# Batching the key transposes and scores ahead of the value product, and moving the projection pieces to even units, in a cached GQA decode kernel

## The chip, the cores and the metric

One core of one Trainium2 (trn2) chip. The metric is the device time of one execution in microseconds (us). A profile's span is about 2 us shorter than the time of the same run (before: 453.79 us and a span of 451.5).

Engines in the profile: PE is TensorE (matmul), PEld its weight loads, DVE VectorE, ACT ScalarE, POOL GpSimd, SP SyncE, which issues the loads. "Warm" and "cold" (or "half clock") stand for a granted TensorE clock of 1.00 and of 0.50 in the windows view of the profile.

## The reference, cut to what matters

Two attention blocks of one decode step stand side by side. Block A attends over 8192 cached positions; block B only over the last 2048.

```python
def block(x, k_cache, v_cache, wq, wo):         # B: caches cut to the last W = 2048 positions
    q = (x @ wq) -> [4 batch, 32 heads, 1, 128]
    k, v = caches [4, 8 kv heads, S, 128], each kv head shared by 4 query heads
    scores = q . k * 128 ** -0.5
    p = softmax(scores)                          # over positions
    return (p . v) reshaped to [4, 1, 4096] @ wo # -> [4, 1, 512]
out = concatenate([block(A), block(B)], axis=-1)
```

This is grouped-query attention (GQA): query heads share a kv head. About nine tenths of the bytes are K and V: 184.56 MB are read per execution.

## The kernel before

The work is cut into 20 units, 0 to 19. A unit owns one 4 MB piece of K and one 4 MB piece of V, in two-slot buffers. TensorE transposes K in 16 steps `T`, and VectorE and ScalarE evict the transposes in turn. TensorE then forms scores in 16 steps `S`, three steps behind. The softmax of unit u-1 is finished during unit u, and so are its row sums `SM` and its value product, 8 chunks `PV` of 16 matmuls. So `PV` inside unit u needs V of unit u-1. Two units make one turn of a loop on TensorE. In seven turns an output projection piece (`OT`, `OL`, `OPJ`; 1 MB of `wo`) is done in the turn's odd unit; the last piece is done after the loop. In the first three turns the same instructions run and their result is not used.

```python
LA, PV0 = 3, 10
TOK = []; pc = 0
for k in range(NJ + LA):                       # NJ = 16
    if k < NJ: TOK.append(("T", k))
    if k >= LA: TOK.append(("S", k - LA))
    if k == PV0 - 1: TOK.append(("SM",))
    if k >= PV0 and pc < NC:                   # NC = 8
        TOK.append(("PV", pc)); pc += 1
AFTER = {("S", 2): ("OT",), ("S", 5): ("OL",), ("S", 8): ("OPJ",)}

for u in range(NU):                            # NU = 20, unrolled for all engines but TensorE
    turn[0] = tn = u // 2
    odd = u % 2 == 1                           # this unit carries the projection piece
    # ... cut: TensorE ops in the order of TOK; PV 0 waits for V of unit u - 1 ...
    for k in range(0, NJ, 2):                  # VectorE, in order
        add(ev[k])                             # eviction of transpose k
        if k == 0 and u >= 1:
            add(dve_submask(u - 1)); add(dve_sub(u - 1, 0))
        if k == 2 and u >= 1: add(dve_sub(u - 1, 1))
        # ... cut ...
        if k == 12 and u >= 1: add(dve_sum(u - 1)); add(dve_rcp(u - 1))
    add(dve_max(u, 1))                         # ... cut: maxc, addmask; POOL all-reduce ...
    if u >= 1: add_norm(u - 1)                 # waits for the last PV chunk
# tail, L = NU - 1 = 19
add(dve_submask(L)); add(dve_sub(L, 0)); add(dve_sub(L, 1)); add(act_exp(L))
op("pe", pe_seed, ...)                         # puts the output so far into two PSUM banks
pe_SM(L)
# ... cut: PV of unit 19 (V comes in 4 chunks), norm, last projection with Wl, store ...

# SyncE: order of loads; each waits until its buffer slot is free
for u in range(1, NU + 1):
    if u < NU: kv_load("K", u)                 # waits for T 15 of unit u - 2
    kv_load("V", u - 1)                        # waits for the last PV of unit u - 3
    if u % 2 == 0 and u // 2 in pieces: load of Wo   # waits for the OPJ of the turn before
```

## Time and profile before

| | before |
|---|---|
| time, median of 3 runs | 453.9 us (453.87 to 454.83) |
| span of the profile | 451.5 us |
| PE busy | 81% |
| DMA queue of the loads, share of 16 engines | 96.3% |

From the page of the kernel before: the DMA busy share and the traffic in 40 equal slices of the span (11.3 us each; digits are tenths), and the line of the queue that carries all loads (packets, MB, share).

```profile
DMA  8999999999999999999999999999999999999950
GB/s 358 406 414 421 420 418 420 422 446 430 422 430 441 427 425 427 436 432 424 430 434 431 427 441 425 427 427 431 437 424 427 437 434 422 433 439 424 409 192 2
...
q1 hardware_dynamic: 12944, 184.56, 96.3%
```

Here is the tail in the timeline of the kernel before. Its columns are start, duration, engine, line, operation, output<-inputs, shapes, count; in brackets is the idle time before it and what ended it. On TensorE, `KT<-identf,K_sb` are transposes of K, `SA` or `SB<-RQc,KT_sb` scores, `SA<-PT,onesb` row sums, `OT<-PT,V_sb` value chunks (`KT<-PT,V_sb` in unit 19's own value product) and `KT<-Wo_sb,OL` a projection piece.

```profile
416.64 3.42 PE L257 MATMUL KT<-identf,K_sb 128*128 128x128 f32 x16 [4.42 <-DMA K_sb<-in_A_k_cache_dram]
...
426.51 0.63 PE L304 MATMUL OT<-PT,V_sb 128*128 128x64 bf16 x16
...
427.72 1.89 PE L367 MATMUL KT<-Wo_sb,OL 128*4 128x512 bf16 x8
...
435.44 0.63 PE L304 MATMUL OT<-PT,V_sb 128*128 128x64 bf16 x16
...
435.90 0.35 PE L290 MATMUL SB<-RQc,KT_sb 128*128 128x16 bf16 x8
436.28 0.69 DVE L396 TENSOR_REDUCE M<-SB 128x8 f32<-128x512 f32 x1 [2.63 <-PE SB L290]
...
438.08 0.69 DVE L434 TENSOR_TENSOR Dt<-SA,MBm 128x512 f32<-128x512 f32 x1
...
439.40 1.06 ACT L443 ACTIVATE PT<-Dt 128x1024 bf16<-128x1024 f32 x1 [4.28 <-DVE Dt L434]
...
440.51 0.78 PE L316 MATMUL SA<-PT,onesb 128*128 128x64 bf16 x16 [2.10 <-ACT PT L443]
...
441.10 5.33 PE L304 MATMUL KT<-PT,V_sb 128*128 128x64 bf16 x128
```

Unit 19 starts when its K lands (416.64). Its first value chunk comes at 426.51, a projection piece at 427.72, the last value chunk at 435.44 and the last scores at 435.90. Only then comes the serial softmax chain: maximum, two subtractions, exponential (to 440.46), the last row sums (440.51) and the last 128 value matmuls. From the waits of TensorE (total us, times, longest):

```profile
PE KT L257 <- DMA K_sb<-in_A_k_cache_dram: 29.5, 7, 4.5
...
PE OT L304 <- DMA V_sb<-in_A_v_cache_dram: 3.8, 5, 1.5
```

### The profile page before, as it was taken

The numbers are of one execution on the slowest core, as the hardware profiler recorded it, in microseconds if no ns is written. First come the engines' busy times: TensorE is split into PE (matmuls) and PEld (weight loads), VectorE is DVE, ScalarE is ACT, GpSimd is POOL, SyncE is SP. The second block draws the span as 40 slices with busy tenths as digits, with TensorE's granted clock in tenths as the row PEclk, the third lists the DMA queues.
The fourth block names the chain that finished last, engine by engine and source line by source line (L and its number), as shares of the span: only waits on it lengthen the run. The fifth ranks groups of instructions, "written<-read, shape, count | busy, mean of one in ns | idle before, by whom it ended". The sixth has DMA issues, their size and how long they took to land.

```text
span 451.5 us, 15657 instructions
## 1 busy us (share of the span) xinstructions
PE 367.6 (81%) x7282; PEld 340.9 (76%) x7282; DVE 207.8 (46%) x473; ACT 182.0 (40%) x183; POOL 21.3 (5%) x56
## 2 busy tenths in 40 slices
PE   0249898988989979896986988698969878986976
PEld 0239878987987978885876878688958878885866
DVE  0134445463663645535463545355445535362641
ACT  1005344552653625443452526163624534351620
POOL 6100000000000000000000000000000000000000
PEclk9999989989999979996999799889969996999898
DMA  8999999999999999999999999999999999999950
GB/s 358 406 414 421 420 418 420 422 446 430 422 430 441 427 425 427 436 432 424 430 434 431 427 441 425 427 427 431 437 424 427 437 434 422 433 439 424 409 192 2
DMA packets 13047, 184.78 MB, mean 409 GB/s; under 512 B 1332, under 2 KB 2408, under 8 KB 4456
## 3 DMA queue, kind: packets, MB, share of 16 engines
q1 hardware_dynamic: 12944, 184.56, 96.3%
q8 instruction: 8, 0.13, 0.1%
q14 instruction: 7, 0.06, 0.0%
q0 software_dynamic: 64, 0.02, 0.0%
q10 hardware_dynamic: 24, 0.01, 0.0%
HBM read 184.56 MB, written 0.01 MB: 409 GB/s over the span
## 4 chain that ended last, share of the span: by engine, by line
DMA 43%; PE 40%; issue 7%; DVE 5%; ACT 4%; SPq 1%; POOL 0%; POOLq 0%
DMA K_sb<-in_A_k_cache_dram 21%; PE KT L257 18%; DMA V_sb<-in_A_v_cache_dram 15%; PE OT L304 10%; DMA K_sb<-in_B_k_cache_dram 7%; PE SB L290 4%; PE KT L367 3%; PE SA L290 2%; ACT PT L443 2%; DVE Dt L434 2%; ACT KT_sb L266 2%; DVE KT_sb L265 1%; PE SA L316 1%; PE KT L304 1%; DVE M L396 1%
## 5 line engine op out<-in xcount | busy, mean ns | idle before, releaser
L266 ACT ACTIVATE KT_sb<-KT 128x1024 bf16<-128x1024 bf16 x160 | 161.2, 1021 | 231.3 <-PE KT L257 231.0
L257 PE MATMUL KT<-identf,K_sb 128*128 128x128 f32 x1280 | 211.8, 301 | 49.2 <-DMA K_sb<-in_A_k_cache_dram 29.5
L257 PEld LDWEIGHTS KT<-identf,K_sb 128*128 128x128 f32 x1280 | 151.9, 153 | 53.0 <-DMA K_sb<-in_A_k_cache_dram 30.2
L265 DVE COPY KT_sb<-KT 128x512 int32<-128x512 int32 x160 | 110.2, 689 | 126.5 <-PE KT L257 126.0
L304 PE MATMUL OT<-PT,V_sb 128*128 128x64 bf16 x2560 | 100.5, 193 | 3.8 <-DMA V_sb<-in_A_v_cache_dram 3.8
L304 PEld LDWEIGHTS OT<-PT,V_sb 128*128 128x128 bf16 x2560 | 84.3, 97 | 8.9 <-DMA V_sb<-in_A_v_cache_dram 4.4
L290 PEld LDWEIGHTS SA<-RQc,KT_sb 128*128 128x128 bf16 x1280 | 56.7, 99 | 6.8 <-ACT KT_sb L266 3.0
L290 PE MATMUL SA<-RQc,KT_sb 128*128 128x16 bf16 x1280 | 57.0, 171 | 1.1
L290 PE MATMUL SB<-RQc,KT_sb 128*128 128x16 bf16 x1280 | 55.8, 170 | 1.3 <-issue 1.3
L290 PEld LDWEIGHTS SB<-RQc,KT_sb 128*128 128x128 bf16 x1280 | 51.7, 97 | 2.5 <-issue 1.4
L396 DVE TENSOR_REDUCE M<-SB 128x8 f32<-128x512 f32 (+1 forms) x20 | 13.8, 691 | 54.1 <-PE SB L290 54.1
L417 POOL PARTITION_ALL_REDUCE MB<-M1m x20 | 7.7, 386 | 400.4 <-DVE M1m L410 400.4
L443 ACT ACTIVATE PT<-Dt 128x1024 bf16<-128x1024 f32 x20 | 21.1, 1054 | 10.1 <-DVE Dt L434 10.1
L367 PE MATMUL KT<-Wo_sb,OL 128*4 128x512 bf16 x80 | 18.9, 379 | 0.0
L188 PE MATMUL KT<-ident,x_sb 4*128 4x4 bf16 x8 | 0.6, 170 | 18.9 <-POOL identf L500 18.9
L316 PE MATMUL SA<-PT,onesb 128*128 128x64 bf16 x336 | 13.6, 195 | 2.1 <-ACT PT L443 2.1
L188 PEld LDWEIGHTS KT<-ident,x_sb 4*128 4x128 bf16 x8 | 0.4, 112 | 19.1 <-issue 19.1
L434 DVE TENSOR_TENSOR Dt<-SA,MBm 128x512 f32<-128x512 f32 x20 | 13.8, 691 | 0.7
L396 DVE TENSOR_REDUCE M<-SA 128x8 f32<-128x512 f32 (+1 forms) x20 | 13.6, 680 | 0.0
L434 DVE TENSOR_TENSOR Dt<-SB,MBm 128x512 f32<-128x512 f32 x20 | 13.6, 680 | 0.0
L316 PEld LDWEIGHTS SA<-PT,onesb 128*128 128x128 bf16 x336 | 11.5, 99 | 2.6 <-ACT PT L443 2.6
L367 PEld LDWEIGHTS KT<-Wo_sb,OL 128*4 128x4 bf16 x80 | 6.0, 84 | 8.1
(68 smaller groups left out, 113.8 us busy)
## 6 DMA issues: line engine op xcount, KB each, us to landing
K_sb<-in_A_k_cache_dram SPq DMA_DIRECT2D x16, 4096.0 KB, 24.0
V_sb<-in_A_v_cache_dram SPq DMA_DIRECT2D x15, 4096.0 KB, 32.0
K_sb<-in_B_k_cache_dram SPq DMA_DIRECT2D x16, 1024.0 KB, 23.7
V_sb<-in_B_v_cache_dram SPq DMA_DIRECT2D x16, 1024.0 KB, 20.5
V_sb<-in_B_wq_dram SPq DMA_DIRECT2D x1, 4096.0 KB, 12.3
V_sb<-in_A_wq_dram SPq DMA_DIRECT2D x1, 4096.0 KB, 21.6
Wo_sb<-in_B_wo_dram SPq DMA_DIRECT2D x4, 1024.0 KB, 18.6
Wo_sb<-in_A_wo_dram SPq DMA_DIRECT2D x3, 1024.0 KB, 18.0
```

What stands on the lines that cost most here:

```text
L188: ins = pe.transpose(out=bk[:, c * 8:c * 8 + Bn], in_=x_sb[0:Bn, P, :].rearrange("b (p c) -> b c p", c=DC)[:, c, :], identity=ident[0:Bn, ...
L257: ins = pe.transpose(out=bkf[:, pi * 128:(pi + 1) * 128], in_=K_sbf[:, slot, t0:t0 + 2, :].rearrange("p t d -> p (t d)"), identity=identf[ ...
L265: return e.tensor_copy(out=KT_sb.bitcast(I32)[:, tj % NKT, :], in_=bkf.bitcast(I32)[:, :])
L266: return e.activation(out=KT_sb[:, tj % NKT, :], in_=bk[:, :], func=ACTF.Copy)
L290: ins = pe.matmul(out=stb[:, t % NTH * C:(t % NTH + 2) * C], lhsT=ktv[:, pi, :, e], rhs=RQc[:, u % 2, t // TS, e, :], start=(e == 0), stop ...
L304: ins = pe.matmul(out=otb[:, s * NW:(s + 1) * NW], lhsT=V_sb[:, slot, t, :], rhs=PT[:, slot, t * C:t * C + NW], start=(j == 0), stop=(j == ...
L316: ins = pe.matmul(out=SA[u % 2][:, s * NW:(s + 1) * NW], lhsT=onesb[:, :], rhs=PT[:, u % 2, c0:c0 + NW], start=(i == 0), stop=(i == n - 1))
L367: ins = pe.matmul(out=bk[0:Bn, 0:D], lhsT=OL[:, i // REP, i % REP, :], rhs=Wo_sb[:, i // REP, i % REP, :], start=(i == 0), stop=(i == C - 1))
L396: return dve.tensor_reduce(out=M1[:, h * n:(h + 1) * n].rearrange("p (s h) -> p s h", h=C), in_=bank[:, :].rearrange("p (s j h) -> p s h j ...
L417: return pool.partition_all_reduce(MB[:, 0:n], M1m[:, 0:n], channels=128, reduce_op=ReduceOp.max)
L434: return dve.tensor_tensor(out=Dt[:, h * NTH * C:(h + 1) * NTH * C].rearrange("p (s j h) -> p s j h", s=Sh, h=C), in0=bank[:, :].rearrange ...
L443: return act.activation(out=PT[:, u % 2, 0:NT * C], in_=Dt[:, :], func=ACTF.Exp, scale=scale)
```

## The change

Its intent: let all transposes and scores of a unit run without the values between them, so that the softmax chain of a unit can overlap the value block of the unit before, and V is needed later. The projection pieces go to the even unit of a turn.

```diff
@@ order of TensorE's work inside a unit
         for k in range(NJ + LA):
             if k < NJ:
                 TOK.append(("T", k))
+            elif k == NJ:
+                TOK.append(("SM",))
+            else:
+                TOK.append(("PV", pc))
+                pc += 1
             if k >= LA:
                 TOK.append(("S", k - LA))
-            if k == PV0 - 1:
-                TOK.append(("SM",))
-            if k >= PV0 and pc < NC:
-                TOK.append(("PV", pc))
-                pc += 1
+        while pc < NC:
+            TOK.append(("PV", pc))
+            pc += 1
@@ the unit that carries the projection piece (the name stays)
-            odd = u % 2 == 1
+            odd = u % 2 == 0
@@ VectorE: row sums and reciprocal move from k == 12 to just ahead of the normalisation
-                if k == 12 and u >= 1:
-                    add(dve_sum(u - 1))
-                    add(dve_rcp(u - 1))
             add(dve_addmask(u))
             if u >= 1:
+                add(dve_sum(u - 1))
+                add(dve_rcp(u - 1))
                 add_norm(u - 1)
@@ tail
-        op("pe", pe_seed, waits=[("ocp", NTURN - 1)])
+        op("pe", pe_seed, waits=[("ocp", NTURN - 1), ("otr", L - 1)])
```

More of the change, by code (lines that the diff above doesn't have):

```diff
@@ L53, in bass_concat_heads__gqa_block_cached__sliding_block_cached__decode_kernel @@
     NTH = NT // 2
-    PV0 = 10
     X = [A_x, B_x]
```

## The prediction

> **What bounds the kernel now.** DMA. The page's slices show the DMA engines 80 to 99% busy from the first slice through slice 38, and the queue table gives 96.3% of the span to the one input queue (184.56 MB). In one-microsecond windows the traffic runs at about 425 GB/s until 434-435 us and then dies; the span is 451.5 us. The list of DMA issues shows that each K and V load is issued while one or two older 4 MB loads (about 9.8 us each) are still in flight, so the queue never runs dry. TensorE is 81% busy but waits for K at unit starts (29.5 us in the waits table). Time = DMA stream (~435 us) + tail (~16.5 us).
>
> **The tail before** (timeline). K of unit 19 lands at 416.64. Unit 19 runs to 436.2: cold clock (granted 0.50) for its first 3.5 us, 16 transposes and scores, the value product of unit 18 interleaved from the eleventh transpose, and a projection piece (1.9 us plus a 0.4 us gap, and about 0.5 us of small transposes). Only then comes the serial softmax chain 436.2 -> 440.5 (max, all-reduce, two subtractions of 0.69, exponential 1.06), row sums and 128 value matmuls to 446.4 (half of them cold), normalise, last projection and store to 451.5.
>
> **What the change does.** It removes no work. (1) Projection pieces move to even units, so unit 19 loses its piece: about -2.5 us. (2) In unit 19 the scores end before six of eight value chunks (16 matmuls = 0.43 us each, read from the 0.66 us score+value steps): max and all-reduce overlap about 2.5 us of them. But the normalisation of unit 18, which waits for the last value chunk, now stands before the subtractions on VectorE, giving back about 1 us. (3) Within all other units the softmax bubble at the unit border (1.3 us "issue" idle, and stalled evictions) is hidden, and V is needed later; the loads are queue-bound, so this is worth nothing. (4) A cost: a piece's weights (1 MB) are queued behind V of the previous unit and land about 2.4 us after it (before: at 406.7, V at 404.3). In an even unit the projection now stalls TensorE there for 3-4 us, seven times. The unit then ends about when the next K lands, so I expect no DMA gap: roughly 10 us of V remain queued.
>
> **Sum.** Unit 19 starts at 416.6-418; a step of transpose+score is 0.68 us, so transposes end near 429, scores near 431, value block 433.4, subtractions 434.2-435.7, exponential 436.8, final value block (probably cold, 5.3 us) to 442.7, plus the unchanged 5.1 us: span about 447.8, 3.7 us less. Time about 450.2 us (-0.8%). V chunks (435.4) and last weights (438.8) land in time.
>
> The Trainium skill, "TensorE: Matmul & The Clock Gate", Part 1, says that the array runs at half clock after an idle window of about 3.4 us. The trace agrees: 0.50 for 3.5 us after the 4.4 us wait at 416.6. If the last value block is warm, another 2 us go.
>
> **Right if:** DMA rate and its end (434-435 us) are unchanged; TensorE idle moves from unit starts to the projection in even units; the last scores end near 431; the distance from there to the end is about 17 us.
> **Wrong if:** the projection stalls accumulate until loads are issued too late (DMA share dips, slower by 1-3%); or unit 18 ends well past 418 so that the tail gain is lost; or DMA had hidden gaps that earlier K issues fill (faster).
>
> Chances: faster by over 2% 0.05, within 2% 0.91, slower 0.04. Range 447.8 to 452.6 us.

## More of the kernel before

DMA is busy from the first slice to the 38th, and the traffic dies in the 39th. The windows view says it with numbers. Its columns are the stretch in us, its length, the busy time of PE, PEld, DVE, ACT and POOL with instruction counts, then the granted clock, the DMA share and GB/s.

```profile
34.00:112.00 78.00, 71.16 (x1377) 65.97 (x1378) 37.09 (x77) 35.14 (x35) 2.70 (x8) 0.96 1.01 423
112.00:434.00 322.00, 276.95 (x5399) 257.79 (x5398) 161.61 (x354) 142.88 (x143) 8.79 (x29) 0.93 1.00 429
434.00:447.00 13.00, 9.18 (x229) 8.21 (x227) 3.76 (x12) 2.08 (x2) 0.37 (x1) 0.87 0.07 25
```

Between 112 and 434 us the DMA share is 1.00 at 429 GB/s. The Trainium skill, "DMA: Bandwidth & Descriptors", section "Where 436 GB/s comes from", works out 435.2 GB/s as the ceiling of the path into SBUF; the measured 429 is 98.6% of it. So the stream sets the time up to 434 us, and what can move is the tail behind it.

## The result

| | before | after |
|---|---|---|
| time, median | 453.88 us (452.89 to 454.83, 4 runs) | 447.01 us (445.83 to 448.14, 4 runs) |
| ratio after/before | | 0.9849 (95% interval 0.9815 to 0.9882) |
| span of the profile | 451.5 us | 446.4 us |

A ratio here is the mean time of one kernel's fast runs over the mean of the other's fast runs of the same rounds, so it is not quite the ratio of the medians. The change is faster by 1.5%, 6.9 us by the medians. I had predicted 3.7 us, and 447.01 lies below my range (447.8 to 452.6). The run that was profiled happened to be the slowest of the four, 448.14 us.

The same page lines after the change (slices of 11.2 us):

```profile
DMA  8999999999999999999999999999999999999990
GB/s 347 415 421 418 421 416 421 421 453 410 442 432 423 423 438 438 435 423 426 426 424 449 432 429 424 423 438 440 423 432 426 426 435 435 432 411 442 421 363 9
```

The same windows after the change:

```profile
34.00:112.00 78.00, 71.92 (x1431) 67.04 (x1431) 41.53 (x85) 38.63 (x39) 2.70 (x8) 1.00 1.02 423
112.00:434.00 322.00, 276.70 (x5423) 252.11 (x5423) 160.86 (x354) 140.87 (x142) 9.16 (x30) 0.94 1.00 429
434.00:447.00 13.00, 8.95 (x160) 8.23 (x160) 1.41 (x5) 0.55 (x2) 0.00 (x0) 0.76 0.07 24
```

The stream has hardly moved: share 1.00 and 429 GB/s in the same stretch, and it ends at the same time (24 GB/s after 434 us, before 25). The last K lands 0.7 us sooner than before (issued at 385.09, 30.8 us to landing: 415.9; before 416.6), but so it does in e10 below (415.9), which has the old order, so that is not an effect of the change. The gain lies in the tail. The same stretch of the timeline:

```profile
415.91 1.97 PE L256 MATMUL KT<-identf,K_sb 128*128 128x128 f32 x16
...
426.97 0.63 PE L303 MATMUL OT<-PT,V_sb 128*128 128x64 bf16 x16
...
428.10 0.35 PE L289 MATMUL SB<-RQc,KT_sb 128*128 128x16 bf16 x8
...
428.30 2.96 PE L303 MATMUL OT<-PT,V_sb 128*128 128x64 bf16 x96
428.48 0.69 DVE L395 TENSOR_REDUCE M<-SB 128x8 f32<-128x512 f32 x1 [2.17 <-PE SB L289]
...
431.30 0.19 DVE L469 TENSOR_REDUCE OS<-OT 128x8 f32<-128x32 f32 x1 [1.15 <-PE OT L303]
...
431.80 0.69 DVE L433 TENSOR_TENSOR Dt<-SA,MBm 128x512 f32<-128x512 f32 x1
...
433.12 1.06 ACT L442 ACTIVATE PT<-Dt 128x1024 bf16<-128x1024 f32 x1 [5.80 <-DVE Dt L433]
...
434.24 1.04 PE L315 MATMUL SA<-PT,onesb 128*128 128x64 bf16 x16 [0.72 <-ACT PT L442]
...
435.08 6.20 PE L303 MATMUL KT<-PT,V_sb 128*128 128x64 bf16 x128
```

Unit 19 starts at 415.91 without a wait, just as its K lands. The first value chunk stands at 426.97, after the last transpose and 1.4 us after V of unit 18 has landed (issued at 390.09, 35.5 us to landing: 425.6); the last scores end at 428.45, before at 436.25. The normalisation of unit 18 (431.30) waits for the value block and holds the subtractions (431.80). The last row sums start at 434.24, before at 440.51. Then, in this profile, 1.1 us are given back: the last sums and values take 7.0 us (434.24 to 441.28) instead of 5.9 (440.51 to 446.43). What is behind that is the same in both: 5.1 us to the end of the span. And the waits of TensorE:

```profile
PE KT L256 <- DMA K_sb<-in_A_k_cache_dram: 19.9, 7, 4.1
PE KT L366 <- DMA Wo_sb<-in_B_wo_dram: 12.5, 4, 4.1
PE KT L366 <- DMA Wo_sb<-in_A_wo_dram: 5.8, 3, 2.2
```

It waits less for K, and 18.3 us for projection weights, which it did not before.

### The profile page after: what moved, and what is told of

It is laid out like the page before. It is cut to its first block, busy times and chain, and to the rows that moved or that the text cites. A ratio compares the mean times of both kernels' runs of the same rounds, so it can differ in the third digit from the quotient of the medians.

```text
span 446.4 us, 15658 instructions
## 1 busy us (share of the span) xinstructions
PE 366.0 (82%) x7282; PEld 335.0 (75%) x7282; DVE 208.7 (47%) x473; ACT 181.5 (41%) x183; POOL 21.3 (5%) x56
## 4 chain that ended last, share of the span: by engine, by line
DMA 54%; PE 36%; DVE 4%; ACT 3%; issue 2%; SPq 1%
DMA Wo_sb<-in_B_wo_dram 27%; DMA Wo_sb<-in_A_wo_dram 13%; PE KT L256 12%; PE OT L303 10%; DMA K_sb<-in_A_k_cache_dram 7%; DMA K_sb<-in_B_k_cache_dram 7%; PE KT L366 5%; PE SB L289 4%; DVE Dt L433 2%; DVE KT_sb L264 2%; ACT PT L442 2%; PE SA L315 2%; PE KT L303 1%; PE SA L289 1%; ACT KT_sb L265 1%
## 5 line engine op out<-in xcount | busy, mean ns | idle before, releaser
L256 PE MATMUL KT<-identf,K_sb 128*128 128x128 f32 x1280 | 204.0, 293 | 32.0 <-DMA K_sb<-in_A_k_cache_dram 19.9
L256 PEld LDWEIGHTS KT<-identf,K_sb 128*128 128x128 f32 x1280 | 145.2, 148 | 42.3 <-DMA K_sb<-in_A_k_cache_dram 21.3
L303 PE MATMUL OT<-PT,V_sb 128*128 128x64 bf16 x2560 | 84.5, 193 | 1.6 <-issue 1.6
L303 PEld LDWEIGHTS OT<-PT,V_sb 128*128 128x128 bf16 x2560 | 78.4, 98 | 1.7 <-issue 1.7
L289 PEld LDWEIGHTS SA<-RQc,KT_sb 128*128 128x128 bf16 x1280 | 55.3, 97 | 5.2 <-ACT KT_sb L265 3.4
L289 PE MATMUL SA<-RQc,KT_sb 128*128 128x16 bf16 x1280 | 56.1, 170 | 1.0
L366 PE MATMUL KT<-Wo_sb,OL 128*4 128x512 bf16 x80 | 25.5, 476 | 18.4 <-DMA Wo_sb<-in_B_wo_dram 12.5
L366 PEld LDWEIGHTS KT<-Wo_sb,OL 128*4 128x4 bf16 x80 | 7.1, 96 | 30.3 <-issue 25.4
## 6 DMA issues: line engine op xcount, KB each, us to landing
Wo_sb<-in_A_wo_dram SPq DMA_DIRECT2D x3, 1024.0 KB, 30.8
```

The lines of the kernel that those rows point to most:

```text
L256: ins = pe.transpose(out=bkf[:, pi * 128:(pi + 1) * 128], in_=K_sbf[:, slot, t0:t0 + 2, :].rearrange("p t d -> p (t d)"), identity=identf[ ...
L289: ins = pe.matmul(out=stb[:, t % NTH * C:(t % NTH + 2) * C], lhsT=ktv[:, pi, :, e], rhs=RQc[:, u % 2, t // TS, e, :], start=(e == 0), stop ...
L303: ins = pe.matmul(out=otb[:, s * NW:(s + 1) * NW], lhsT=V_sb[:, slot, t, :], rhs=PT[:, slot, t * C:t * C + NW], start=(j == 0), stop=(j == ...
L366: ins = pe.matmul(out=bk[0:Bn, 0:D], lhsT=OL[:, i // REP, i % REP, :], rhs=Wo_sb[:, i // REP, i % REP, :], start=(i == 0), stop=(i == C - 1))
```

## The experiments

The theory, called the tail theory: all of the gain lies behind the landing of the last K, and the rest of the program hides behind the DMA stream. Two rivals: the stream theory (K loads, now issued earlier, fill gaps of the DMA) and the bubble theory (the softmax bubble at every unit border was on the path).

### e0: the change again

No edit, as the measure on the same chip.

> The changed kernel unedited, so that the other runs of this call have it on the same chip. Every theory: 447 us, between 445.5 and 448.5.

Measured: 448.1 us (447.17 to 449.46, 4 runs), ratio 0.9882 (0.9867 to 0.9897). As expected, but 1.1 us slower than the first time. In its profile the projection of unit 18 ran partly on a half clock (0.50 from about 407.5 us; 2.56 us for 8 matmuls instead of 1.89), and unit 19 started at 417.20 instead of 415.91.

### e1: only the pieces move

```diff
 # the kernel before
-            odd = u % 2 == 1
+            odd = u % 2 == 0
```

> Only the projection pieces move to even units; the kernel before otherwise. Tail theory (all of the gain lies after the last K has landed): unit 19 loses its 2.3 to 2.8 us piece, and unit 18 now ends late enough that unit 19 starts warm (up to 1.7 us more): 449.5 to 451.5 us. Stream theory (K loads issued earlier fill gaps of the DMA): the transposes end as late as before, so 453 to 454. Bubble theory (the softmax bubble at every unit border was on the path): the bubble is still there, 453 to 454.

Measured: 452.56 us, ratio 0.9985 (0.9969 to 1.0002): 0.3 us by the medians and 0.7 by the ratio, so I missed, and the time alone would side with the rivals. The timeline of unit 19 in e1 shows what happened:

```profile
415.95 1.97 PE L257 MATMUL KT<-identf,K_sb 128*128 128x128 f32 x16 [1.10 <-DMA K_sb<-in_A_k_cache_dram]
...
422.75 0.63 PE L257 MATMUL KT<-identf,K_sb 128*128 128x128 f32 x4
...
423.22 0.35 PE L290 MATMUL SA<-RQc,KT_sb 128*128 128x16 bf16 x8
...
425.67 1.03 PE L304 MATMUL OT<-PT,V_sb 128*128 128x64 bf16 x16 [2.11 <-DMA V_sb<-in_A_v_cache_dram]
...
426.52 1.09 PE L257 MATMUL KT<-identf,K_sb 128*128 128x128 f32 x4
...
434.52 0.35 PE L290 MATMUL SB<-RQc,KT_sb 128*128 128x16 bf16 x8
```

As I had expected, unit 19 has no piece and starts warm: its first 16 transposes take 1.97 us instead of 3.42. It gets to the first value chunk about 3 us sooner than before, finds that V of unit 18 has not landed, and waits 2.1 us, until 425.67; the clock has dropped by then, and the next transposes are slow (1.09 instead of 0.63). All later transposes and scores stand behind that chunk, and the last scores end at 434.87, only 1.4 us sooner than before. There is a second gate behind the one that the edit opens: the landing of V. In the kernel before it lay about 0.2 us ahead of the first value chunk. An estimate says so: 9.72 us from the landing of the last K to that of V, from e1, added to 416.64 gives 426.36, and the chunk started at 426.51. The trace of the kernel before agrees: V of unit 18 is issued at 394.59 and lands 31.7 us later, at 426.3. So it showed as no wait at all.

### e2: only the block order

```diff
 # the change
-            odd = u % 2 == 0
+            odd = u % 2 == 1
```

> Only the block order of the change; the pieces stay in odd units. Tail theory: unit 19 keeps its piece (2.3 us) and starts cold after a wait for K (1.7 us), and only the overlap of the softmax chain with the value block is gained: 450 to 452 us. Stream theory and bubble theory: the whole gain, 446 to 448.

Measured: 451.65 us, ratio 0.9979 (0.9962 to 0.9997), as the tail theory expected. Unit 19 in e2:

```profile
416.25 3.41 PE L256 MATMUL KT<-identf,K_sb 128*128 128x128 f32 x16 [4.98 <-DMA K_sb<-in_A_k_cache_dram]
...
426.40 1.89 PE L366 MATMUL KT<-Wo_sb,OL 128*4 128x512 bf16 x8
```

It waits 5 us for K and starts cold (3.41 us), then pays for its piece (1.89 us). The last scores end at 433.09, 16.8 us after the start; in the change it is 12.5. So each half of the change alone is worth about 1 us or less, and both together 5 to 7. One more thing shows in e2: the nine gaps of TensorE called "issue" at transposes are still there (10.9 us in all; 11.5 in the kernel before), so the block order does not hide them.

### e5: K issued late

```diff
-w = [("T", tjob_idx[(u - 2, NJ - 1)])] if kind == "K" else ...
+w = [("PV", (u - 3) * NC + NC - 1)] if kind == "K" else ...
```

> The changed kernel with each large K load held back until the value block of the same unit is done (about 5 us later than in the change, and as late as V). Tail and bubble theories: older loads are still in flight, DMA busy share stays 1.00 between 112 and 434 us, 446.5 to 448 us. Stream theory: the gain of the change goes, 452 to 454.

Measured: 446.98 us (445.93 to 448.98), ratio 0.987, DMA share 1.00 between 112 and 434. The stream theory falls: K issued as late as V (unit 19's at 389.04; in the change 385.09) costs nothing. In odd units that is still earlier than in the kernel before (392.59), so it is as telling that the share was 1.00 before the change too: there were no gaps to fill.

### e6: more TensorE work in every unit

```diff
+            reps = 1 if turn[0] is None else 4
-                for s in range(NSEG):
+                for s in [s for _ in range(reps) for s in range(NSEG)]:
```

> The changed kernel with the row-sum matmuls done four times in each unit of the loop (about 1.3 us more TensorE work in each of 20 units, same result). Tail theory: TensorE has slack in all units but the last, so only unit 19 (and perhaps unit 18) pays: 448 to 450 us. Bubble theory: TensorE time is on the path in every unit: about 20 to 26 us more, 467 to 473.

Measured: 449.78 us, ratio 0.9925 (0.9898 to 0.9952). About 28 us of added work (an estimate: 20 units of 1.4 us, since the sums take 2.03 us in unit 19 instead of 0.62) cost 2 to 3 us, and 1.4 of them lie in unit 19 itself. The bubble theory falls: TensorE time inside the stream is free.

### e7: projection weights ahead of V

```diff
-            kv_load("V", u - 1)     # was ahead of Wo
             tn = u // 2
             # ... cut: load of Wo, unchanged ...
+            kv_load("V", u - 1)     # is now behind it
```

> The changed kernel with the 1 MB of projection weights queued ahead of V instead of behind it. The projection in even units then waits for nothing (the change waits 18.3 us there in all, seven times). Tail theory: those waits lie off the path; the last K lands at 415.9 as before, unit 18 now ends near 412, so unit 19 starts after a wait of about 4 us on a cold clock, and its last scores come about 1 us later: 447.3 to 449.3 us, no gain. If the waits were on the path: 5 to 15 us faster than the change.

Measured: 447.51 us (445.38 to 448.32, 6 runs), ratio 0.9867. The 18.3 us of waits for weights are gone from its profile, and the time is that of the change, so those waits lie off the path. My mechanism for it was wrong: unit 18 ended at 413.8, the wait for K was 2.04 us and not 4, and unit 19 started warm. The first transposes of unit 19 and the last value block in e7:

```profile
415.80 1.97 PE L256 MATMUL KT<-identf,K_sb 128*128 128x128 f32 x16 [2.04 <-DMA K_sb<-in_A_k_cache_dram]
...
434.61 3.90 PE L303 MATMUL KT<-PT,V_sb 128*128 128x64 bf16 x128
```

Here the last value block, after the same idle time as in the change, ran warm: 3.90 us instead of 6.20. It ran warm in the profiles of e5 and e6 too, which also have the tail of the change.

### e3, e4, e8: three edits of the tail

The seed is `pe_seed` of the tail, small matmuls that put the output so far into the banks of the last projection. e3 adds fill matmuls to keep the clock up; e4 puts the two subtractions of unit 19 ahead of the normalisation of unit 18; e8 does both.

```diff
 # e3 (5 ahead of the seed, 4 behind; e8 has 3 behind)
+ins = pe.matmul(out=KTB[1][:, :], lhsT=onesb[:, :], rhs=PT[:, (L - 1) % 2, 0:512], start=True, stop=True)
 # e4 and e8
-                add_norm(u - 1)
+                if u < L:
+                    add_norm(u - 1)
         add(dve_sub(L, 1))
+        add_norm(L - 1)
-  pe_seed waits=[("ocp", NTURN - 1), ("otr", L - 1)]
+  pe_seed waits=[("ocp", NTURN - 1), ("sum", L - 1)]
```

> The changed kernel plus nine matmuls of 512 columns into an unused bank (about 0.22 us each), between the value block of unit 19 and the last row sums, where TensorE idles 3.0 us. If the idle gap is what drops the granted clock to 0.50, the last sums and values (7.0 us in the trace of the change, all cold) take 3.6 to 4 us: 443 to 444.5 us. If the clock has another cause: no change, 447, or 0.3 us more.

> The changed kernel with, in the last unit only, the two subtractions ahead of the normalisation of unit 18 on VectorE. The exponential should start 1.3 to 1.5 us earlier: 445.4 to 445.8 us. If VectorE order does not matter there: 447.

> Both edits of the tail: subtractions first, and three fill matmuls of 512 columns after the seed of the output. TensorE then idles under 1 us before the last sums[...]: gains add, 442 to 443.5 us. Not below about 441, since the last projection weights land near 438 us and the last projection, copy and store take 4 us or so more.

Measured: e3 447.23 us (ratio 0.9863), e4 446.68 (0.9857), e8 446.48 (0.9856). The intervals overlap with that of the change: inconclusive, and all three are misses. The timeline of e8 tells why:

```profile
431.81 1.06 ACT L442 ACTIVATE PT<-Dt 128x1024 bf16<-128x1024 f32 x1 [4.27 <-DVE Dt L433]
...
432.69 0.59 PE L644 MATMUL SA<-oacc,identf 4*4 4x256 f32 x2 [1.21 <-issue]
...
433.64 0.82 PE L650 MATMUL KT<-PT,onesb 128*128 128x512 bf16 x3
...
434.30 0.63 PE L315 MATMUL SA<-PT,onesb 128*128 128x64 bf16 x16
```

The exponential starts at 431.81 as planned (the change: 433.12) and ends at 432.87, but the seed, though it waits for nothing any more, starts 1.2 us after the value block ("issue"), and with the fill it now holds the last sums until 434.30. That gap is the end of TensorE's loop: it lies between the last matmul of the loop and the first behind it, and in e4, which has the same gap, the trace shows the ten semaphore instructions that close a turn issued from 430.6 to 432.0, and the seed next, at 432.48. In e3 a gap of 1.1 us and the fill pushed the sums 1.2 us past the exponential. So e4 and e8 did bring the exponential forward, and a new queue on TensorE ate part of it. The last value block took 3.90 us, warm, in the profiles of all three; but e4 has no fill, and e5, e6 and e7 were warm without it, so it is not shown that the fill did that.

### e9 and e10: does the landing of V hold e1 back?

Both load only half of V of unit 18, a wrong result (relative error 0.079). e9 is e1 with this edit, e10 the kernel before with it.

```diff
+            nt = NT // 2 if kind == "V" and u == L - 1 else NT
-... ap=[[NT * DH, 128], [1, NT * DH]]  ->  buf[:, slot, :, :]
+... ap=[[NT * DH, 128], [1, nt * DH]]  ->  buf[:, slot, 0:nt, :]
```

> Wrong result on purpose: pieces in even units in the old order (as e1), and V of unit 18 loaded only by half (2 MB less), so that it lands about 4.9 us earlier. If the landing of V of unit 18 is what held e1 back (its first value chunk waited until 425.7), the last scores come near 430.6 instead of 434.7: about 4 us faster than e1, 447.5 to 449.5 us. If it was not: 451.5 to 453.

> Wrong result on purpose: the kernel before with the same half load of V of unit 18, the control of the run above. There the first value chunk of unit 19 comes at 426.5, just after V lands, so an earlier V frees nothing; the DMA stream ends about 5 us earlier, and if the end followed the stream it would be 448. Expected: 452.5 to 454 us, the same as the kernel before.

Measured: e9 449.39 us, ratio 0.9901 (0.9876 to 0.9927); e10 453.67 us, ratio 0.9997 (0.9971 to 1.0024). Both as expected. In e9 the first value chunk (424.04) waits for nothing, and the last scores end at 431.88, 3.0 us sooner than in e1:

```profile
424.04 0.63 PE L304 MATMUL OT<-PT,V_sb 128*128 128x64 bf16 x16
...
431.53 0.35 PE L290 MATMUL SB<-RQc,KT_sb 128*128 128x16 bf16 x8
```

So moving the pieces is worth about 4.5 us (by the ratio), if V is not in the way; and an earlier V, or a stream that is 2 MB shorter, is worth nothing to the kernel before (e10).

### e13: is the block needed?

The old interleaved order with pieces in even units, and the first value chunk three transposes later.

```diff
 # e1
-    PV0 = 10
+    PV0 = 13
-        for k in range(NJ + LA):
+        for k in range(NJ + LA + 2):
-            if k >= LA:
+            if LA <= k < NJ + LA:
```

> The kernel before with pieces in even units (e1) and the first value chunk three transposes later (still interleaved, correct result). If what matters is that the first value chunk comes after V has landed (425.7 in e1), and not that the values form one block, the last scores come near 431 to 432 instead of 434.9 and the time is 448.5 to 450 us. If the block as such is needed: 452 to 453 us, as e1.

Measured: 447.94 us (446.58 to 448.82), ratio 0.9866 (0.9839 to 0.9893), even better than expected and as good as the change. Unit 19 in e13:

```profile
417.20 1.94 PE L257 MATMUL KT<-identf,K_sb 128*128 128x128 f32 x16
...
426.69 0.63 PE L304 MATMUL OT<-PT,V_sb 128*128 128x64 bf16 x16
...
430.75 0.35 PE L290 MATMUL SB<-RQc,KT_sb 128*128 128x16 bf16 x8
...
435.50 1.04 PE L316 MATMUL SA<-PT,onesb 128*128 128x64 bf16 x16 [0.86 <-ACT PT L443]
```

The first value chunk, at 426.69, comes after the landing of V and waits for nothing. The last sums start at 435.50. In the profile of e0, the change, unit 19 also starts at 417.20 and the last sums also start at 435.50. So the value block as such buys nothing here: its scores end sooner (429.72 in e0, 431.10 in e13), but the normalisation, which waits for the whole value block and stands ahead of the subtractions on VectorE, gives that back.

### e11 and e12: a shorter tail

e11 has the subtractions first (as e4), drops half of the seed (VectorE adds that half of the output at the end) and puts the other half behind the last values. e12 is e11 with the weights ahead of V (as e7).

```diff
 # e11, beside the edits of e4
-            for hf in range(2):                      # seed, was ahead of pe_SM(L)
+            for hf in range(1, 2):                   # now behind the last PV
-    start=False, stop=(hq == C - 1)
+    start=(hf == 0 and hq == 0), stop=(hq == C - 1)
-dve.tensor_copy(out=osb[:, 0, 0:H2], in_=halves[0])
+dve.tensor_tensor(out=osb[:, 0, 0:H2], in0=halves[0], in1=oacc[:, 0, 0:H2], op=AluOpType.add)
```

> The changed kernel, tail only: subtractions ahead of the normalisation; half of the output seed dropped (VectorE adds it at the end), the other half after the last values. TensorE then idles 1.6 us instead of 3 before the last sums, and those start at about 432.9 instead of 434.2 (profile of the change). Expected 443.5 to 446 us, 2 to 3 us faster than the change, with the last value block warm in most runs. If the start of the last sums is not on the path: 447.

> The short tail (e11) with the projection weights queued ahead of V (e7). In the profile of e11 unit 19 started at 417.3, because unit 18 ended late after its wait for weights on a half clock; in that of e7 at 415.8, when the last K landed. If that lateness is on the path and common: 443.5 to 444.8 us, about 1 us faster than e11. If it is rare or off the path: 445.3.

Measured: e11 445.26 us, ratio 0.9809 (0.9782 to 0.9836); e12 444.89 us (444.28 to 445.61), ratio 0.9806 (0.9782 to 0.983). Both give the right result. Both beat both kernels: in the call of e11 the kernel with the tail of the change (e7) had 447.51, and the interval of e0 (0.9867 to 0.9897) lies clear of both; that of the change's first call (0.9815 to 0.9882) overlaps theirs. e11 came out as expected. e12 against e11 is inconclusive: 0.4 us by the medians, but the same by the ratios. From the timeline of e11: the projection of unit 18, the last row sums, the last values:

```profile
406.34 3.36 PE L366 MATMUL KT<-Wo_sb,OL 128*4 128x512 bf16 x8 [1.46 <-DMA Wo_sb<-in_A_wo_dram]
...
434.08 0.64 PE L315 MATMUL SA<-PT,onesb 128*128 128x64 bf16 x16 [1.45 <-ACT PT L442]
...
434.56 3.90 PE L303 MATMUL KT<-PT,V_sb 128*128 128x64 bf16 x128
```

The last sums start at 434.08 (I had expected 432.9) although unit 19 started as late as 417.31; in e0, with a start at 417.20, they start at 435.50.

### The tails side by side

Read from the timelines of the profiles, in us. The change and e0 are the same kernel. Each row is one run: both profiled runs of the change were the slowest of their four, that of e7 the fastest of its six.

| | unit 19 starts | last scores end | exponential ends | last sums start | last values end | span |
|---|---|---|---|---|---|---|
| before | 416.64 | 436.25 | 440.46 | 440.51 | 446.43 | 451.5 |
| e1 | 415.95 | 434.87 | 439.08 | 439.13 | 445.00 | 450.1 |
| e2 | 416.25 | 433.09 | 438.83 | 438.88 | 444.80 | 449.9 |
| change | 415.91 | 428.45 | 434.18 | 434.24 | 441.28 | 446.4 |
| e0 | 417.20 | 429.72 | 435.45 | 435.50 | 442.59 | 447.7 |
| e7 | 415.80 | 428.34 | 434.08 | 434.13 | 438.51 | 443.6 |
| e13 | 417.20 | 431.10 | 435.44 | 435.50 | 441.08 | 446.2 |
| e11 | 417.31 | 429.82 | 434.03 | 434.08 | 438.46 | 443.5 |
| e12 | 416.48 | 429.01 | 433.23 | 433.28 | 437.65 | 442.7 |

## Why the prediction was right or wrong

**Right: what bounds the kernel.** The stream was to stay as it was and end at 434 to 435 us. It did, by the windows, and e5 and e6 show that neither earlier loads nor TensorE time inside the stream counts. It was also right that the waits for weights in even units cost nothing (e7). They are 18.3 us in all, 2.6 each, where I had put 3 to 4.

**Wrong in size: the length of the last unit.** The term that failed reads "transposes end near 429, scores near 431, value block 433.4". Measured: transposes 426.3, scores 428.45, value block 431.26. The start was 415.91 where I had 416.6 to 418, and from the start to the last scores it took 12.5 us (in both profiles of the change) where my numbers give 13 to 14.4. My single figures fit a start at 418: sixteen full steps of 0.68 us from there end at 428.9. So about 2.1 of the 2.5 us at the last scores are the start. Unit 18 waited 1.70 us for its weights and not 3 to 4, and ran on a full clock straight into unit 19 just as K landed; in e0, where it waited 2.05 us and the clock fell, unit 19 started at 417.20 and the scores ended at 429.72. The rest, 0.4 to 0.5 us, is in the steps: the first four transposes run back to back in 1.8 us without scores between them, where four steps would be 2.7. Of these 2.5 us the last sums and values took back 1.1: I had 5.9 us for them, and the profile shows 7.0. The rest of the miss in the profiled run, about 0.6 us, is outside the span: I had added 2.4 us to the span to get the time, as before, and here the two differ by 1.7. Against the median the miss is 3.2 us; the other 1.1 is that the profiled run was slower than the median, and those runs have no profile.

**Not in the sum: two outcomes of the clock.** The last value block ran cold in both profiles of the change (granted clock 0.50; 7.0 us with its sums) and warm in e5, e6 and e7, which have the same tail and nearly the same idle time (4.4 us with its sums in e7). I had it as "another 2 us go" if warm; the runs show 2.7. This is the likely reason why times of the change reach from 445.83 to 449.46; it was seen in profiles, not in every run, and so is not shown.

**Wrong in cause: how the gain is made.** I had added up two gains, "about -2.5 us" for the piece that leaves unit 19 and an overlap of about 2.5 us less 1 us given back, and had written of the bubble and the later need for V in all other units: "this is worth nothing". The landing of V as a gate in unit 19 is not in my prediction at all. Alone, the first is worth 0.3 to 0.7 us (e1) and the second about 1 us (e2); together they give 5 to 7. The parts don't add because two gates stand in series in unit 19. The landing of the last K and the piece fix how soon the unit gets to its first value chunk; the landing of V, 9.7 us after K, fixes when that chunk may start, and in the old order everything behind it waits too. Before the change the second gate opened 0.2 us ahead of the moment at which the work got there. To open one alone gains next to nothing; e9 (V earlier, 449.4 us against 452.6) and e13 (values later, 447.9 us) show the second one. So the later need for V, which I had set to zero elsewhere and left out of unit 19, is what lets the other part pay.

**Misread: the bubble.** I had called the 1.3 us "issue" gaps a softmax bubble that the block order hides. They stand at the first unit of a turn, they stay in e2, and in the kernel before the ten semaphore instructions that close a turn are issued there (from 394.1 to 395.4 at the turn that starts at 395.96). They are the end of TensorE's loop. In the stream they cost nothing, so the sum did not suffer.

**Not shown.** How the gap of 1.2 us at the loop's end divides between the ten semaphore instructions and the rest was not tested. What decides between a warm and a cold last block is not known from these runs.

## What to carry to other kernels

When a trace shows no wait at a point, ask how near the next gate was: compare the time at which the data lands with the time at which the work got there, for a gate that is met by 0.2 us holds as fast as one that is waited for, once the work ahead of it speeds up. In a kernel bound by its load stream, follow only the work behind the last landings, put work that can wait for data last among the ready work there, and hang side work (here the projection piece) on a unit whose time is covered by the stream. Two edits that are each worth 1 us or less can be worth 1.2 to 1.5% together, so a step that changes next to nothing by itself is no proof that it is useless.

## What the Trainium skill lacked or had wrong

- "TensorE: Matmul & The Clock Gate", Part 1 and the table "Why this matters for your kernels": the advice is to avoid idle gaps of TensorE over about 3 us. Here shorter gaps were followed by the half clock: 1.46 us ahead of the projection in e11 (clock 0.79 in the next window of 1 us and 0.50 in the three after it; the 8 matmuls took 3.36 us instead of 1.89) and 2.05 us in e0 (2.56 us), while 1.70 us in the change and 2.04 us in e7 were not. The page does say that its window runs freely; these numbers show that the length of the gap alone does not decide.
- "Advanced Engine Details and Errata", section "Control Flow Timing": a compare-and-branch is given as about 108 ns. The nine gaps called "issue" at transposes, 11.5 us in all, in the kernel before, and the 1.2 us behind the loop's last value block in e4 and e8, show about ten times that at the end of a turn of TensorE's loop. It is no figure for the branch alone: ten semaphore instructions of 51 ns close a turn here, issued over 1.4 us that reach into the gap. No page has a figure for a turn's end as a whole.
- "DMA: Bandwidth & Descriptors", section "Where 436 GB/s comes from": its ceiling agrees, 429 GB/s on one core against 435.2. Its remark that for transfers between HBM and SBUF the HBM side binds, at about 358 GB/s, does not hold for the one core measured here, which read from HBM at 429.
